# A GEGLU block on one core: the down projection of three pairs of hidden blocks by seven products for eight

## The chip, the core and the metric

The kernel runs on one core of a Trainium2 chip. A core has a matrix engine (TensorE, PE in the profile; PEld is its loading of weights), a vector engine (VectorE, DVE), a scalar engine (ScalarE, ACT), GpSimd (POOL) and a queue that issues transfers (SyncE, SP). Matrix products land in PSUM, eight banks of 128 partitions x 512 values of fp32, and are read from there by VectorE and ScalarE. The metric is the device time of one execution in microseconds; three runs of the kernel before gave 1671.05 us as their median (1670.72 to 1672.84).

## The reference

The block is a transformer layer on 2048 rows of 512 values, with 32 heads of attention over the last 512 keys and then a gated feed-forward part. `mod` holds six rows of 512 made from a condition vector; `gb` is the last of them.

```python
h = _layernorm(x, axis=-1) * (1 + ca) + sa
x = x + ga * _A_ref(h, A_k_cache, A_v_cache, A_wq, A_wo)     # attention
h = _layernorm(x, axis=-1) * (1 + cb) + sb
x = x + gb * _B_ref(h, B_w_gate, B_w_up, B_w_down)

def _B_ref(x, w_gate, w_up, w_down):
    g = jnp.einsum("bsd,df->bsf", x, w_gate)
    u = jnp.einsum("bsd,df->bsf", x, w_up)
    h = _gelu(g) * u
    return jnp.einsum("bsf,fd->bsd", h, w_down)
```

The hidden width is 1376. The change is in the last line of `_B_ref`, the down projection.

## The kernel before

**Numbers.** All products of fp32 values are made from fp16 parts: an operand is split into a high part (a rounding to fp16) and a low part (the rest), and a product of two operands is three matmuls, high x high, high x low and low x high. So what is called a product below is always three matmuls for each block of the inner dimension. The splits are an `activation` with Copy on ScalarE for the high part and a subtraction for the low part.

**Tiling of the feed-forward part.** The 2048 rows are four groups of 512 (`qg`), taken in two pairs `p` = 0 and 1. The hidden width is cut into NF = 11 blocks `f` of 128, of which the last, block 10, has 96. A unit `(p, f)` makes the hidden values of one block for the 1024 rows of a pair, transposed: 128 hidden values on the partitions, rows along the free dimension. The gate and up projections of a unit are made with Winograd's form of Strassen's scheme, seven products where a plain 2 x 2 scheme has eight, in four stages (`stage(u, k)`, k = 0 to 3), 42 matmuls of 512 columns in all. `finish(u, r)` multiplies the gelu by the up values for each of the two groups r on VectorE, and `hid_high` and `hid_low` split the result into the tile `hid`.

**The down projection.** Hidden blocks are taken two at a time. Once both units of such a couple are done, `down_put` puts eight entries into a list `DQ`, one for each of the pair's eight tiles of 128 rows. `down` takes one entry after each stage of the units that follow: `down_mm` issues six matmuls (two blocks, three each) of 512 columns, `hid` as the weights that are loaded and `w_down` as the operand that streams, into one bank of psO or psW, and `down_add` adds the bank to the accumulator of that tile of rows, `acc[t]`, on VectorE (one SCALAR_TENSOR_TENSOR of 128 x 512). The last addition of a tile is followed by its output transfer. `w_down` is loaded once, gated with `gb` and split once (`wd_load`, `wd_gate`, `wd_high`, `wd_low`), and kept.

The units come in the order of `UNITS`: all of p = 0 with p = 1's blocks 6 to 9 among them, then (0, 10), then (1, 0) to (1, 5), and (1, 10) last. So the couples (0, 1), (2, 3) and (4, 5) of p = 1 are made last, over the final 110 us or so. At the very end there are the couple (4, 5) and block 10 for all eight tiles: for tiles 4 to 7 of the pair the couple's and block 10's matmuls go into one bank and are added once, for tiles 0 to 3 they are two groups.

**Who sets the order.** The program does not run in the order in which it is written. The class `Weaver` records every call, lets a planner with costs for each engine play the whole program through, and issues the instructions of each engine in the order that it found. Each engine then works through its list strictly in that order, and waits on semaphores where an operand isn't there yet or a buffer isn't free. A low part or a sum written with `tt` may go to GpSimd or VectorE, as the planner chooses. All instructions stand on line 418, the call in `Weaver.issue`, so the profile's rows are told apart by the names of tiles: `psS` holds the units' products, `psO`, `psW` (two banks) and `psQ` the down projection's, `aw` the gate and up weights, `hid` the hidden values, `wd` w_down, `r` and `h` what lies between, `acc` the accumulators.

## Time and profile before

| | |
|---|---|
| median of three runs | 1671.05 us (1670.72 to 1672.84) |
| profiled execution, its own time | 1670.47 us |
| its span, first to last instruction | 1668.7 us |
| mean granted clock of TensorE | 0.998 |
| TensorE busy | 1658.7 us, 99% of the span |
| VectorE, ScalarE, GpSimd busy | 1265.9, 1220.4, 1232.5 us |

A row of a group in the profile reads: engine, operation, output <- inputs, count | busy time in all and mean ns of one | idle time of the engine ahead of these instructions, and what ended it. A row of the timeline gives start, duration, engine, operation, shapes, count, and in brackets the idle time before it. The duration of a matmul reaches to the end of its way through the array, so a stream of them goes faster than their durations say; the pitch of the weight loads shows the rate.

### The profile page before, as it was taken

How to read it: one execution, taken by the hardware profiler on the slowest of the kernel's cores; microseconds unless marked ns; L12 is line 12 of the kernel's file. 1: busy time of each engine (PE TensorE's matmuls, PEld its weight loads, DVE VectorE, ACT ScalarE, POOL GpSimd, SP SyncE). 2: the span in 40 equal slices, each digit the busy share in tenths (PEclk: the TensorE clock that was granted, in tenths of full speed). 3: DMA queues.
4: the chain of work that ended last, by engine and by line, in shares of the span. 5: the costliest groups of instructions: out<-in, count | busy, mean ns of one | idle time of the engine just before them, and what ended most of it. 6: DMA issues, size and time to landing. Idle time of an engine off the chain costs nothing.

```text
span 1668.7 us, 24116 instructions
## 1 busy us (share of the span) xinstructions
PE 1658.7 (99%) x7750; PEld 765.0 (46%) x7750; DVE 1265.9 (76%) x2374; ACT 1220.4 (73%) x2423; POOL 1232.5 (74%) x1013
## 2 busy tenths in 40 slices
PE   8999999999999999999999999999999999999999
PEld 5444444444444444444444444444444444444444
DVE  7877777778787877787888888777777966665555
ACT  6977778877877777878787878687777876545541
POOL 4878898867675767676666789999867898875530
PEclk9999999999999999999999999999999999999999
DMA  8778679977677767786989787879777712111111
GB/s 239 143 142 152 114 123 177 180 133 161 134 148 126 146 121 149 125 149 122 175 183 195 164 163 163 153 152 184 139 141 138 137 41 64 42 30 34 34 38 51
DMA packets 666351, 217.11 MB, mean 130 GB/s; under 512 B 581552, under 2 KB 648112, under 8 KB 666224
## 3 DMA queue, kind: packets, MB, share of 16 engines
q1 hardware_dynamic: 666224, 215.57, 65.0%
q8 instruction: 61, 1.00, 0.3%
q14 instruction: 66, 0.54, 0.1%
HBM read 68.68 MB, written 4.19 MB: 44 GB/s over the span
## 4 chain that ended last, share of the span: by engine, by line
PE 98%; DVE 1%; ACT 1%; DMA 0%; SPq 0%; issue 0%; DVEq 0%
PE psS L418 32%; PE psW L418 24%; PE psO L418 23%; PE psQ L418 18%; DMA wm<-in_w_mod_dram 0%; SPq L418 0%; ACT acc L418 0%; DVE st L418 0%; DVE acc L418 0%; ACT B L418 0%; ACT p L418 0%; DVE sc L418 0%; DVE q L418 0%; DVE mx L418 0%; ACT h L418 0%
## 5 line engine op out<-in xcount | busy, mean ns | idle before, releaser
L418 POOL TENSOR_TENSOR pp<-p,pp 128x1024 f16<-128x1024 f32 x256 | 545.4, 2130 | 269.8 <-ACT pp L418 161.7
L418 ACT ACTIVATE p<-psS,st,es 128x512 f32<-128x512 f32 x512 | 393.0, 773 | 168.0 <-DVE st L418 167.1
L418 DVE SCALAR_TENSOR_TENSOR acc<-psW,st,acc 128x512 f32<-128x512 f32 x496 | 367.9, 742 | 120.5 <-PE psW L418 118.7
L418 PE MATMUL psW<-wo,oT 128*128 128x512 f16 x1536 | 415.1, 379 | 0.0
L418 PE MATMUL psS<-kT,q 128*128 128x512 f16 x1536 | 383.9, 379 | 0.0
L418 PE MATMUL psO<-pT,v 128*128 128x512 f16 x1536 | 374.0, 379 | 0.0
L418 DVE TENSOR_REDUCE st<-psS 128x2 f32<-128x1024 f32 x256 | 312.7, 1221 | 60.3 <-PE psS L418 59.5
L418 ACT ACTIVATE pp<-p 128x1024 f16<-128x1024 f32 x256 | 271.2, 1059 | 3.8
L418 PEld LDWEIGHTS <-v 128*128 128x128 f16 x1536 | 150.2, 98 | 180.4 <-issue 0.5
L418 PEld LDWEIGHTS <-oT 128*128 128x128 f16 x1536 | 150.3, 98 | 180.1
L418 PEld LDWEIGHTS <-q 128*128 128x128 f16 x1536 | 147.5, 98 | 170.9 <-issue 1.1
L418 ACT ACTIVATE oT<-psO 128x512 f16<-128x512 f32 x128 | 76.0, 594 | 88.6 <-PE psO L418 88.1
L418 PE MATMUL psQ<-B,A 128*128 128x512 f16 x528 | 128.8, 380 | 0.1
L418 PEld LDWEIGHTS <-aw 128*128 128x128 f16 (+1 forms) x840 | 84.3, 100 | 96.0
L418 PE MATMUL psS<-T,aw 128*128 128x512 f16 (+1 forms) x480 | 116.3, 379 | 0.0
L418 PEld LDWEIGHTS <-A 128*128 128x128 f16 x756 | 74.5, 99 | 89.4 <-issue 1.9
L418 PE MATMUL psQ<-T,S 128*128 128x512 f16 x468 | 113.7, 379 | 0.0
L418 DVE SCALAR_TENSOR_TENSOR oT<-psO,oT 128x512 f16<-128x512 f32 x128 | 88.1, 689 | 32.9 <-ACT oT L418 32.6
L418 ACT ACTIVATION_READ_ACCUMULATOR p<-psS,st,es 128x1 f32 x512 | 101.5, 198 | 0.0
L418 PEld LDWEIGHTS <-S 128*128 128x128 f16 x624 | 61.0, 98 | 73.6
L418 DVE TENSOR_TENSOR r<-psS,h 128x512 f32<-128x512 f32 (+1 forms) x60 | 40.9, 688 | 69.5 <-ACT h L418 37.2
L418 DVE TENSOR_REDUCE mx<-raw 128x1 f32<-128x512 f32 x128 | 85.9, 675 | 9.5 <-DMA raw<-in_A_k_cache_dram 4.7
(210 smaller groups left out, 2264.6 us busy)
## 6 DMA issues: line engine op xcount, KB each, us to landing
raw<-in_A_k_cache_dram SPq DMA_DIRECT2D x32, 256.0 KB, 3.8
raw<-in_A_wq_dram SPq DMA_DIRECT2D x32, 256.0 KB, 3.3
raw<-in_A_v_cache_dram SPq DMA_DIRECT2D x32, 256.0 KB, 3.2
raw<-in_A_wo_dram SPq DMA_DIRECT2D x32, 256.0 KB, 3.0
pT<-pp SPq DMA_TRANSPOSE x512, 3.2
raw<-in_B_w_gate_dram SPq DMA_DIRECT2D x24, 256.0 KB, 3.1
raw<-in_B_w_up_dram SPq DMA_DIRECT2D x24, 256.0 KB, 3.1
raw<-in_B_w_down_dram SPq DMA_DIRECT2D x20, 256.0 KB, 2.9
```

The source lines that it names most:

```text
L418: made[n] = real(*a, **k)
```

## The change

For p = 1, the couples (0, 1), (2, 3) and (4, 5) (`PAIRS`) make the down projection in the same form of seven products for eight. The 2 x 2 scheme is: two groups of 512 rows, by two hidden blocks, by two halves of 256 output columns. One product is a matrix of 128 hidden values x 512 rows with a matrix of 128 x 256 of w_down.

- `finish` for these units only writes the multiplied values to a tile `hf` of fp32 (both groups). `pa_split` and `pa_sums` make from them the seven operands A11, A12, A22, S1 to S4: four sums of 128 x 512 and seven splits. They live in the tiles B11, T2, T1, B22 and so on of the gate and up part, which are free by then; for the couple (2, 3) in slots of `hid`.
- `wt_make` loads the two blocks of `w_down` again, gates them, makes the four differences of halves on GpSimd or VectorE, and splits the result into a tile `WT` (T3, T4 and B21 by couple).
- `pair_step` issues one step n of `CHAIN` for one half j of the rows (two tiles of 128): six matmuls of 256 columns into a bank that holds two tiles by 256 columns, and one addition on VectorE of 128 x 2 x 256 into a quarter of the result. There are two banks for each j, psW and psO for j = 0 and psW and psQ for j = 1. The steps 0, 2, 4 and 6 add up in one of them and 1; 3 and 5 use the other; a step that goes on in a bank waits until the addition of the step before has read it.
- For the last couple (`LAST`) the chain has ten steps in the order 0, 1, 2, 3, 4, 5, 7, 8, 6, 9. Steps 6 to 9 carry block 10: step 6 adds it to the seventh product's bank, 7, 8 and 9 have block 10 alone. They end with the output transfers, of 2 x 128 rows by 256 columns.
- The accumulators become one tile of 128 x 16 x 512, so that an addition can reach two tiles of rows. Scale factors are shifted by powers of two, and a count in the planner goes by columns.

In numbers of instructions: 168 matmuls of 512 columns go (with their 168 weight loads), 300 of 256 columns come. Additions on VectorE are 112 for 92.

```diff
@@
-HID = 2.0 ** 38
+HID = 2.0 ** 40
@@ def done
-        return sum(1.0 if ends[n] < until else 0.0 for n, e in enumerate(by) if e == "PE" and self.ops[n][3] == N)
+        return sum(self.ops[n][3] / N if ends[n] < until else 0.0 for n, e in enumerate(by) if e == "PE" and self.ops[n][3] > P)
@@
-    acc = [base.tile([P, D], F32, name=f"acc{t}", tag=f"acc{t}") for t in range(SQ // P)]
+    rows_ = base.tile([P, SQ // P, D], F32, name="acc")
+    acc = [rows_[:, t, :] for t in range(SQ // P)]
@@
+    PAIRS = {(1, f) for f in (0, 2, 4)}
...
+    def pa_split(p, f, nm):
+        src = {"A11": (f, 0), "S3": (f, 1), "A12": (f + 1, 0), "A22": (f + 1, 1), "S1": (f + 1, 1), "S2": (f, 0),
+               "S4": (f + 1, 0)}[nm]
+        t, v = pa_part(p, f, nm), HF[p, src[0]][:, src[1], :]
+        nc.scalar.activation(t[:, 0, :], v, AF.Copy)
+        tt(t[:, 1, :], v, t[:, 0, :], OP.subtract)
+
+    def pa_sums(p, f):
+        (a11, a21), (a12, a22) = [[HF[p, f + k][:, r, :] for r in range(2)] for k in range(2)]
+        pa_split(p, f, "A12")
+        pa_split(p, f, "A22")
+        tt(a22, a21, a22, OP.add)
+        tt(a21, a11, a21, OP.subtract)
+        tt(a11, a22, a11, OP.subtract)
+        pa_split(p, f, "S1")
+        pa_split(p, f, "S3")
+        tt(a12, a12, a11, OP.subtract)
+        pa_split(p, f, "S2")
+        pa_split(p, f, "S4")
+
+    def wt_make(f):
...
+            nc.sync.dma_start(t, w_down[(f + k) * P:(f + k + 1) * P, :])
+            tt(t, t, gb, OP.mult)
...
+    CHAIN = (("A11", 0, 0, 0, 0), ("A12", 1, 0, 0, 0), ("S2", 1, 1, 1, 0), ("S3", 0, 1, 1, 1), ("S1", 0, 0, 1, 1),
+             ("A22", 1, 0, 1, 0), ("S4", 1, 1, 0, 1), (None, 0, 1, 1, 1), (None, 0, 0, 0, 0), (None, 0, 0, 1, 0))
+    NEW = {0: 0, 1: 1, 3: 1, 7: 1, 8: 1, 9: 1}
+    LAST = (1, 4)
+
+    def pair_step(p, f, n, j):
+        nm, k, half, r, c = CHAIN[n]
+        if n in NEW:
+            PX["d", NEW[n], j] = bank(("psW", ("psO", "psQ")[j])[NEW[n]], (2, 1)[NEW[n]])
+        pd = PX["d", int(n in (1, 3, 5, 7, 8, 9)), j].rearrange("p (t c) -> p t c", t=2)
...
+                for i, (x_, y_) in enumerate(((0, 0), (0, 1), (1, 0))):
+                    nc.tensor.matmul(pd[:, t, :], a[:m, x_, js], w[:m, y_, :], start=n in NEW and (t, o, i) == (0, 0, 0),
+                                     stop=(o, i) == (len(ops) - 1, 2), skip_group_check=True)
+        g = 8 * p + 4 * r + 2 * j
+        v = rows_[:, g:g + 2, HALF[c]]
+        nc.vector.scalar_tensor_tensor(v, pd, ffs[:, 5:6], v, op0=OP.mult, op1=OP.add)
+        if ends:
+            nc.sync.dma_start(out[g * P:(g + 2) * P, :].rearrange("(t p) d -> p t d", p=P)[:, :, HALF[c]], v)
@@ def finish
+        if (p, f & ~1) in PAIRS:
+            if u not in HF:
+                HF[u] = right.tile([P, 2, N], F32, name="hf", tag="p32", bufs=2)
+            nc.vector.scalar_tensor_tensor(HF[u][:, r, :], t[:, 1, :], ffs[:, 4:5], t[:, 0, :], op0=OP.mult, op1=OP.mult)
+            if r == 0:
+                if f % 2 == 0:
+                    pa_split(p, f, "A11")
+                else:
+                    pa_sums(p, f - 1)
+            return
@@ the units' loop
+        if u in PAIRS:
+            wt_make(f)
         for k in range(4):
             stage(u, k)
             down()
...
-            if u == UNITS[-2]:
-                down_put(p, (h, h + 1), (0, 1, 2, 3))
+            if (p, h) in PAIRS:
+                DQ.extend((p, "pair", (h, n)) for n in ((0, 1, 2, 3, 4, 5, 7, 8, 6, 9) if (p, h) == LAST else range(7)))
             elif u != UNITS[-1]:
                 down_put(p, (h, h + 1) if h + 1 < NF else (h,))
     down(len(DQ))
-    pds = {}
...
-    down_put(1, (NF - 1,), (0, 1, 2, 3))
-    down(4)
```

Up to about three quarters of TensorE's list its order is the same as before. What it issues behind the last stage of the last unit, before; each of these matmuls stands three times with its weight load, for the three parts, and the sequence goes through tiles of rows, of which three are shown (wd 3101, 3129 and 3220 are the blocks 4, 5 and 10, hid 3379 and 3380 the two groups of block 4):

```order
L418 MATMUL psW_3410<-wd_3101,hid_3380 128x512
L418 MATMUL psW_3410<-wd_3129,hid_3392 128x512
L418 MATMUL psO_3414<-wd_3101,hid_3379 128x512
L418 MATMUL psO_3414<-wd_3129,hid_3391 128x512
L418 MATMUL psO_3414<-wd_3220,hid_3403 128x512
L418 MATMUL psO_3418<-wd_3220,hid_3404 128x512
```

And now, the chain of the couple (4, 5) in the order of its steps, j = 0 but for the second row; each stands six times with its load (B11, T2, T1 and B22 now hold A and S operands, B21 the new weights, wd 3086, 3114 and 3205 are the blocks 4, 5 and 10):

```order
L418 MATMUL psW_3409<-wd_3086,B11_1_3382 128x256
L418 MATMUL psW_3410<-wd_3086,B11_1_3382 128x256
L418 MATMUL psO_3411<-wd_3114,T2_1_3392 128x256
L418 MATMUL psW_3409<-B21_1_3370,T1_1_3393 128x256
L418 MATMUL psO_3413<-B21_1_3370,B11_1_3382 128x256
L418 MATMUL psO_3413<-B21_1_3370,T2_1_3392 128x256
L418 MATMUL psO_3415<-wd_3205,hid_3407 128x256
L418 MATMUL psO_3417<-wd_3205,hid_3408 128x256
L418 MATMUL psW_3409<-wd_3114,B22_1_3394 128x256
L418 MATMUL psO_3419<-wd_3205,hid_3407 128x256
```

Behind the last stage stand 99 matmuls of 512 columns before, and 150 of 256 now. The bank psW_3409 carries four steps, with an addition on VectorE to be waited for between each.

VectorE's list before, from the addition that ends the last unit's stages (`r<-psS`) on, in part:

```order
L418 TENSOR_TENSOR r_3396<-psS_3394,h32_3398 96x512
L418 SCALAR_TENSOR_TENSOR acc15_85<-psO_3405,ffs_95,acc15_85 128x512
L418 SCALAR_TENSOR_TENSOR r_3396<-r_3396,ffs_95 96x512
L418 SCALAR_TENSOR_TENSOR acc8_78<-psW_3406,ffs_95,acc8_78 128x512
L418 SCALAR_TENSOR_TENSOR r_3401<-r_3401,ffs_95 96x512
L418 SCALAR_TENSOR_TENSOR acc9_79<-psW_3407,ffs_95,acc9_79 128x512
L418 TENSOR_TENSOR hid_3403<-r_3401,hid_3403 96x512
```

And now, the same addition and what stands from the multiply `r_3404` on, some rows of evictions between them left out:

```order
L418 TENSOR_TENSOR r_3399<-psS_3397,h32_3402 96x512
L418 SCALAR_TENSOR_TENSOR acc_70<-psQ_3412,ffs_80,acc_70 128x2x256
L418 SCALAR_TENSOR_TENSOR B21_1_3370<-raw_3369,ffs_80,B21_1_3370 128x512
L418 SCALAR_TENSOR_TENSOR r_3404<-r_3404,ffs_80 96x512
L418 SCALAR_TENSOR_TENSOR acc_70<-psW_3409,ffs_80,acc_70 128x2x256
L418 SCALAR_TENSOR_TENSOR acc_70<-psO_3413,ffs_80,acc_70 128x2x256
L418 TENSOR_TENSOR hid_3407<-r_3404,hid_3407 96x512
L418 SCALAR_TENSOR_TENSOR r_3399<-r_3399,ffs_80 96x512
L418 SCALAR_TENSOR_TENSOR acc_70<-psQ_3414,ffs_80,acc_70 128x2x256
L418 SCALAR_TENSOR_TENSOR acc_70<-psO_3415,ffs_80,acc_70 128x2x256
L418 TENSOR_TENSOR hid_3408<-r_3399,hid_3408 96x512
```

Behind the first row there are 21 instructions before and 28 now; the last unit's multiplies and low parts have moved from the front of the stretch to its middle and end.

GpSimd's list before ends with the low parts of the last unit's gate and up weights (`aw`):

```order
L418 TENSOR_TENSOR aw_3369<-raw_3329,aw_3369 128x384
L418 TENSOR_TENSOR aw_3369<-S2f_3366,aw_3369 128x192
L418 TENSOR_TENSOR aw_3369<-S1f_3365,aw_3369 128x192
L418 TENSOR_TENSOR aw_3369<-S3f_3367,aw_3369 128x192
L418 TENSOR_TENSOR aw_3369<-S4f_3368,aw_3369 128x192
L418 TENSOR_TENSOR aw_3369<-raw_3330,aw_3369 128x192
```

Now the operands of the last couple stand behind them:

```order
L418 TENSOR_TENSOR aw_3367<-S4f_3366,aw_3367 128x192
L418 TENSOR_TENSOR B11_1_3382<-hf_3381,B11_1_3382 128x512
L418 TENSOR_TENSOR raw_3369<-raw_3369,raw_3368 128x256
L418 TENSOR_TENSOR raw_3369<-raw_3369 128x256
L418 TENSOR_TENSOR hf_3391<-hf_3381,hf_3391 128x512
L418 TENSOR_TENSOR hf_3381<-hf_3381 128x512
L418 TENSOR_TENSOR hf_3381<-hf_3391,hf_3381 128x512
L418 TENSOR_TENSOR T1_1_3393<-hf_3381,T1_1_3393 128x512
L418 TENSOR_TENSOR T1_1_3393<-hf_3391,T1_1_3393 128x512
L418 TENSOR_TENSOR hf_3391<-hf_3391,hf_3381 128x512
L418 TENSOR_TENSOR B22_1_3394<-hf_3391,B22_1_3394 128x512
```

The splits (names with two equal ends) and the sums (`hf`) take turns, and each sum needs the one before.

55 lines of the change are left out of this document (47 added, 8 removed).

## The prediction

> **What bounds the kernel now.** I read the page's busy shares first, then what TensorE waits for, then the last third of the span by stage, then single rows of its end.
>
> ```profile
> PE 1658.7 (99%) x7750; PEld 765.0 (46%) x7750; DVE 1265.9 (76%) x2374; ACT 1220.4 (73%) x2423; POOL 1232.5 (74%) x1013
> ...
> PE 98%; DVE 1%; ACT 1%; DMA 0%; SPq 0%; issue 0%; DVEq 0%
> ...
> PE psO L418 <- DVE acc L418: 0.4, 1, 0.4
> ```
>
> The second row is the chain that ended last: TensorE alone. The third is the only wait of TensorE from 1380 us to the end: 0.4 us in 289. So until here nothing but the number and length of its matmuls sets the time, and a removed matmul is worth its full length as long as no new wait stands in its place. The stages (core 0; PE, PEld, DVE, ACT, POOL busy, clock, DMA share, GB/s):
>
> ```profile
> 1550.00:1600.00 50.00, 50.00 (x233) 22.67 (x232) 29.53 (x43) 26.09 (x54) 30.26 (x41) 1.00 0.13 45
> 1600.00:1640.00 40.00, 40.00 (x187) 18.86 (x186) 22.43 (x33) 14.26 (x27) 5.24 (x9) 1.00 0.02 7
> 1640.00:1669.00 29.00, 24.63 (x115) 11.27 (x112) 16.09 (x24) 1.94 (x3) 0.00 (x0) 0.99 0.20 73
> ```
>
> The clock is full, the queues carry little, and VectorE, ScalarE and GpSimd are at 50 to 60% and fall off towards the end. All that the change adds goes into these stages, so what matters is whether the cover there is as wide as it looks. The very end, row by row:
>
> ```profile
> 1657.99 6.15 PEld L418 LDWEIGHTS <-hid 128*128 128x128 f16 x29
> 1659.29 1.46 PE L418 MATMUL psW<-wd,hid 96*128 96x512 f16 x6
> 1659.49 0.75 DVE L418 SCALAR_TENSOR_TENSOR acc<-psO,ffs,acc 128x512 f32<-128x512 f32 x1 [4.43 <-PE psO L418]
> 1660.15 1.40 DVE L418 SCALAR_TENSOR_TENSOR acc<-psW,ffs,acc 128x512 f32<-128x512 f32 x2
> 1663.82 0.81 PE L418 MATMUL psO<-wd,hid 96*128 96x512 f16 x3
> 1664.72 0.74 DVE L418 SCALAR_TENSOR_TENSOR acc<-psO,ffs,acc 128x512 f32<-128x512 f32 x1
> ```
>
> From these I take four prices. A matmul of 512 columns with its weight load: 29 loads in 6.15 us, the last 0.10 long, so 6.05/28 = 0.216 us. One eviction of VectorE in a row of several: 1.40 - 0.74 = 0.66 us. From a matmul's last column to the eviction that reads it: the last matmul starts at 1663.82 + 2 x 0.216 = 1664.25, streams to 1664.47, and is read from 1664.72: 0.21 to 0.25 us. And the drain: last eviction ends at 1665.46, the span at 1668.7, so 3.2 us for the last output transfer. Ahead of 1659.49 VectorE stands idle for 4.4 us; it is far from a bound there.
>
> **The change, part by part.** TensorE first. The three pairs of blocks and block 10 of the second pair of row groups lose 168 matmuls of 512 columns (3 x 48 + 24) and get 300 of 256 (3 x 84 + 48). In columns that is 18 x 512 less. The trace has no matmul of 256 columns, so its price is bounded. From below by half of 0.216, 0.108: fixed parts can't be smaller. From above by the load and the stream one after the other, 0.098 + 0.108 = 0.206, if nothing overlaps. The rows nearest to it are a weight load behind a short matmul:
>
> ```profile
> 1380.11 0.27 PE L418 MATMUL psQ<-ident,T 128*128 128x128 f32 x1
> 1380.11 0.21 PEld L418 LDWEIGHTS <-aw 128*128 128x128 f16 x2
> 1380.21 0.38 PE L418 MATMUL psS<-B,aw 128*128 128x512 f16 x1
> 1382.53 0.66 PE L418 MATMUL psQ<-ident,T 128*128 128x128 f32 x4
> 1384.97 0.60 PE L418 MATMUL psQ<-ident,T 128*128 128x128 f32 x4
> ...
> L418 PEld LDWEIGHTS <-hid 128*128 128x128 f16 x480 | 47.0, 98 | 56.1 <-issue 0.7
> ```
>
> The load for the next matmul begins when the one before it begins (1380.11 both), and that next matmul begins 0.10 us later: the load's 98 ns and hardly more. So a pair of load and matmul can follow each 0.10 to 0.11 us, and 256 columns need 0.108. Four transposes of 128 columns in a row, whose loads are of the slower 32-bit kind, keep a pitch of (0.60 - 0.27)/3 = 0.11 us, in the other row (0.66 - 0.27)/3 = 0.13. I take 0.109, by the row that has the same kind of load. Then 300 x 0.109 = 32.8 against 168 x 0.216 = 36.3: **-3.5 us** (ends: -3.9, and +25.5 with no overlap, which these rows rule out).
> The Trainium skill ("TensorE: Matmul & The Clock Gate", section "Wait — 56ns, not 53.3ns?") has a rule that speaks against the change: with the hardware's decoder off, firmware spends about 62 ns on each matmul. If a weight load cost as much again, an estimate by that page is 124 ns a pair, and the TensorE term would be +0.9 instead of -3.5 us; the 0.10 us between 1380.11 and 1380.21 doesn't bear it out, though one pair alone may have been decoded ahead.
>
> VectorE: 112 evictions for 92, since each product is added to one or two quarters of the result on its own: +20. Six weight roundings (low parts) come, twelve low parts of the hidden block move to GpSimd. Net +14 instructions, 14 x 0.66 = +9 us over the last 110 us. In the windows from 1550 to 1640 that is cover enough (52 of 90 us busy). At the end it is not. I count from the last matmul of the last unit's four stages, where in the changed order 150 matmuls of 256 columns are left: 150 x 0.109 = 16.4 us for TensorE. Behind the addition that reads that last matmul VectorE has 28 instructions, 29 with it, 29 x 0.66 = 19.1 us. Before, the same stretch held 99 matmuls of 512 (21.4 us) and 21 instructions of VectorE after that addition. So **the bound changes hands there**. In time: TensorE's last column would fall at 1664.47 - 3.5 = 1660.96 with no wait, the stages' last matmul at 1660.96 - 16.4 = 1644.6; VectorE begins its 29 at 1644.8 and is done at 1644.8 + 19.1 + 0.1 = 1664.0 at the earliest, against 1660.96 + 0.2 + 0.7 = 1661.9 if TensorE set it: **+2.1 us**. The banks force it upon TensorE: each pair of halves lives in one of two banks of psW and in psO and psQ, and step n+2 writes on in the bank that step n's eviction still reads.
>
> Inside those 19 us VectorE also waits once for another engine. The last unit's hidden block takes the way multiply (VectorE), high part (ScalarE), low part (VectorE), and the matmuls of block 10 wait for it:
>
> ```profile
> 1645.93 0.74 DVE L418 SCALAR_TENSOR_TENSOR r<-r,ffs 96x512 f32<-96x512 f32 x1
> 1646.59 0.74 DVE L418 SCALAR_TENSOR_TENSOR acc<-psW,ffs,acc 128x512 f32<-128x512 f32 x1
> 1646.71 0.63 ACT L418 ACTIVATE hid<-r 96x512 f16<-96x512 f32 x1 [1.95 <-DVE r L418]
> 1647.37 0.69 DVE L418 TENSOR_TENSOR hid<-r,hid 96x512 f16<-96x512 f32 x1
> ```
>
> 0.74 + 0.63 + 0.69 = 2.1 us with the two handovers; before, it was done by 1650.5, 8 us ahead of need, now its multiplies stand 8 and 17 places behind the stages' end, and in the changed order only one or two evictions lie between its links. Between 0 (all covered) and 2 x 2.1 I take **+0.6 us**, near the lower end, since there are evictions to run meanwhile.
>
> GpSimd and ScalarE: per pair 7 splits in two halves (ScalarE Copy 0.63, GpSimd subtraction), 4 sums, and for the weights 2 gates and 4 half-wide differences. On GpSimd that is 21 low parts, 12 sums, 6 gates and 12 half-wide differences, while 12 scalings go over to ScalarE: with the prices below at most 39 x 1.29 + 12 x 0.75 = 59 us. I cost it at nothing: from 1550 to 1655 GpSimd stood idle for 20 + 35 + 15 = 70 us; if that cover goes, TensorE waits for the sums (rival below). The prices it goes by:
>
> ```profile
> L418 POOL TENSOR_TENSOR T<-hf,T 128x512 f16<-128x512 f32 x6 | 7.8, 1306 | 2.9 <-DVE r L418 2.9
> L418 POOL TENSOR_TENSOR hf<-hf,ft 128x512 f32<-128x512 f32 x2 | 2.5, 1274 | 0.0
> L418 POOL TENSOR_TENSOR aw<-S4f,aw 128x256 f16<-128x256 f32 x11 | 8.3, 751 | 4.4 <-DVE hid L418 3.6 <-DVE r L418 0.7
> out_dram<-acc SPq DMA_DIRECT2D x9, 256.0 KB, 2.1
> ```
>
> Six more loads of w_down (256 KB each) lie in a stage where the queues are at 13%: nothing. The last output transfers carry as many bytes in rows half as long; between 0 and another 2.1 us I take +0.1, since the bytes are the same. One tile for all accumulators changes names, not waits; new scale factors are other constants: nothing.
>
> Sum: -3.5 + 2.1 + 0.6 + 0.1 = **-0.7 us** on the span: 1668.7 to 1668.0. The profiled execution took 1670.47, 0.6 below the median of the three runs, 1671.05. On that median: **1670.3 us**. Some 0.2% (3.3 us) is about what a measurement of this kernel can tell from no change.
>
> **Rivals.** *All of the gain arrives.* VectorE keeps up because evictions run earlier than I count, and the end follows TensorE: -3.5 + 0.1 gives 1667.6 us, just past 0.2%. For it: 4.4 us of idle VectorE before 1659.49. Against it: 29 instructions of 0.66 in 16.4 us don't fit in any order.
>
> *GpSimd is late: slower.* In the last pair the sums begin when both halves of block 5 are multiplied, by my count 6 us after the last unit's first stage (the two multiplies are the 8th and 9th of VectorE's instructions from there, 9 x 0.66). From there GpSimd does two low parts, a half-wide difference, three sums and three low parts in a row, 8 x 1.27 + 0.75 = 10.9 us, then a sum, ScalarE's Copy and the last low part, 1.27 + 0.63 + 1.3 = 3.2 us more: ready at 17 and 20 us. TensorE wants these operands at about 19 and 23.5. So there are 3 us of slack, after a stretch in which GpSimd is more than 80% busy by count (from the weights of the unit of block 2 on, 41 instructions of some 1.2 us and 40 narrow ones of 0.65: 75 us of work in 88). If it comes 7 us late at the end, or 2.5 us past its slack at each of the three pairs, TensorE waits 4 to 7 us: 1670.3 + 4 to 7 = 1674 to 1677 us. It decides from 4 us of waits upward (1670.3 + 4.1 is the 0.2% bound). Against it: GpSimd's own waits in this stretch before are mostly for ScalarE, it isn't backed up.
>
> *Short pairs can't follow at 0.109: slower.* If the 300 pairs go at the 0.13 us of the dearer row of transposes, TensorE's stream is 300 x 0.021 = 6.3 us longer than I count, and VectorE's surplus of 2.1 us covers so much of it: 1670.3 + 4.2 = 1674.5 us. From 0.127 us a pair on it is slower by over 0.2%. Against it stands the load of the right kind, 0.10 us. The firmware rule of the Trainium skill would be a cause of it.
>
> **How the numbers follow.** The forecast (the gain given back to VectorE at the end) 0.66; all of the gain 0.08; GpSimd late 0.20; dear pairs 0.06. Faster 0.08 (the first rival), same 0.66 (the forecast), slower 0.26 (the last two). Range: from 1667.5 (all gained) to 1676.0, which leaves out the far end of the GpSimd case; the forecast alone gives 1668.5 to 1673.0, from waits of 0 to 4.2 us where I took 0.6.
>
> **What would show it.** Matmuls 128x256 at a pitch of 0.109 in the weight loads' rows; 16.4 us of them behind the last stage, stretched to 18 or 19 by waits of psW, psO and psQ for VectorE's acc, each 0.1 to 0.9 us, 2 to 3 us in total; evictions 128x2x256 of 0.74 us standing back to back to the end; no waits of TensorE for GpSimd. Wrong if TensorE waits in the middle of the units (from 1550 on), or if the evictions in two pieces are dearer than those of 512 in one: at a pitch of 0.80 for 0.66 the end moves by 24 x 0.14 = 3.4 us.

## The result

The changed kernel takes 1673.2 us (median of 21 executions, 1672.66 to 1676.85), the kernel before on the same chip 1670.78 us (21 executions). The ratio is 1.0016, with a 95% interval of 1.001 to 1.0022: the change costs 2.4 us. The forecast was 1670.3 us. The profiled execution took 1672.93 us, its span is 1671.1 us against 1668.7 before. The executions of a kernel can lie in two groups: here 15 of 21 take 1672.7 to 1673.7 us and six 1674.3 to 1676.9, and in the spliced kernel below six of 11 take 1671.2 to 1672.0 and five 1673.0 to 1673.5.

What the change was for did happen. First the busy times, then weight loads of the last stretch (start, duration, engine, operation, count):

```profile
PE 1656.4 (99%) x7882; PEld 777.5 (47%) x7882; DVE 1273.7 (76%) x2384; ACT 1240.3 (74%) x2454; POOL 1279.5 (77%) x1052
```

```profile
1646.64 2.06 PEld L418 LDWEIGHTS <-hid 128*128 128x128 f16 x18
1648.71 1.30 PEld L418 LDWEIGHTS <-B 128*128 128x128 f16 x12
```

TensorE is busy 2.3 us less. Twelve loads of 0.10 us in 1.30 us are a pitch of (1.30 - 0.10)/11 = 0.109 us: a matmul of 256 columns with its load costs what was forecast, and 300 of them for 168 of 0.216 are worth the -3.5 us. VectorE has 7.8 us more, where the forecast had 9. So 5.9 us must have come from somewhere. I cut the span at two points which both kernels have: the opening ends with the first matmul psO<-pT,v (50.56 us before, 50.57 after), and the last matmul of the last unit's stages gives way to the next one at 1643.10 before and 1646.85 after. The rows that begin there, before and then after:

```profile
1643.10 0.81 PE L418 MATMUL psO<-wd,hid 128*128 128x512 f16 x3
1646.85 1.47 PE L418 MATMUL psW<-wd,hid 128*128 128x256 f16 x12
```

| | before | after | difference | of it less or more TensorE work | rest |
|---|---|---|---|---|---|
| opening | 50.56 | 50.57 | 0.0 | 0 | 0.0 |
| from there to the last stage's end | 1592.54 | 1596.28 | +3.74 | +1.5 | +2.2 |
| from there to the span's end | 25.60 | 24.25 | -1.35 | -5.0 | +3.7 |

The work column comes from the counts of matmuls: behind the last stage stand 99 of 0.216 us (21.4 us) before and 150 of 0.109 (16.4 us) now, so -5.0 us there; the whole change is -3.5, so +1.5 lies ahead. The last column is what is lost: 2.2 us ahead of the last stage's end and 3.7 us behind it. With -3.5 that is the measured +2.4.

**The loss upstream.** All waits of TensorE between 1280 and 1500 us in the changed kernel (what waits, for what: us in total, times, longest):

```profile
PE psQ L418 <- ACT hf L418: 1.2, 1, 1.2
PE psS L418 <- ACT r L418: 0.5, 1, 0.5
PE psS L418 <- DVE r L418: 0.3, 1, 0.3
```

In the kernel before there is one wait of 0.4 us there. The stretches (PE, PEld, DVE, ACT, POOL busy, clock, DMA share, GB/s), of the kernel before and then of the changed one:

```profile
1280.00:1400.00 120.00, 120.00 (x586) 58.34 (x585) 91.72 (x169) 93.56 (x175) 103.42 (x103) 1.00 0.45 89
1400.00:1500.00 100.00, 99.59 (x465) 45.33 (x463) 63.96 (x85) 52.45 (x100) 78.17 (x84) 1.00 0.15 41
```

```profile
1280.00:1400.00 120.00, 118.83 (x578) 57.37 (x577) 88.35 (x164) 95.33 (x178) 99.88 (x97) 1.00 0.44 87
1400.00:1500.00 100.00, 99.11 (x462) 45.12 (x461) 59.04 (x80) 55.62 (x106) 82.89 (x90) 1.00 0.16 42
...
1600.00:1640.00 40.00, 40.00 (x247) 24.64 (x246) 26.26 (x39) 19.54 (x36) 35.50 (x41) 1.00 0.16 59
```

TensorE loses 1.17 + 0.48 = 1.65 us of busy time in two stretches that lie ahead of the first matmul of the new scheme (it starts at 1585 us). A wait costs some 0.16 us more than that shows, since a single matmul of 512 columns is recorded with 0.38 us and takes 0.216 in a stream; with two waits more than before that makes 2.0 of the 2.2 us, as an estimate. In the stretch where GpSimd has most of its new work, 35.50 of 40 us, TensorE loses nothing. What happens at the 1.2 us wait can be read row by row. The kernel before, where the scaling of normalized rows (`hf<-psQ`, which empties the bank for the next four transposes) is done by VectorE:

```profile
1344.13 0.60 PE L418 MATMUL psQ<-ident,B 128*128 128x128 f32 x4
1344.84 0.81 DVE L418 TENSOR_SCALAR hf<-psQ,cols 128x512 f32<-128x512 f32 x1 [0.92 <-PE psQ L418]
1345.70 0.66 PE L418 MATMUL psQ<-ident,B 128*128 128x128 f32 x4
```

And the changed kernel, where the same scaling is on ScalarE's list, behind a load of its tables (which the kernel before has too, at 1344.54) and another read of products:

```profile
1344.83 0.60 PE L418 MATMUL psQ<-ident,B 128*128 128x128 f32 x4
1344.97 1.28 ACT L418 ACT_TABLE_LOAD   x1
1346.27 0.69 ACT L418 ACTIVATE r<-psS,ffs 128x512 f32<-128x512 f32 x1
1346.86 0.77 ACT L418 ACTIVATE hf<-psQ,cols 128x512 f32<-128x512 f32 x1
1347.68 0.66 PE L418 MATMUL psQ<-ident,B 128*128 128x128 f32 x4 [1.17 <-ACT hf L418]
```

The bank is full at 1345.43 and is read only from 1346.86. The diff touches no line of this part. The planner plays the whole program through, and for the changed program it found another order, in which such a scaling changes its engine.

**The loss at the end.** TensorE's waits from 1640 us on, in the changed kernel:

```profile
PE psQ L418 <- DVE acc L418: 0.7, 1, 0.7
PE psW L418 <- DVE acc L418: 0.5, 2, 0.3
PE psW L418 <- DVE B L418: 0.4, 1, 0.4
PE psO L418 <- DVE hid L418: 0.2, 1, 0.2
PE psO L418 <- DVE acc L418: 0.2, 1, 0.2
```

All are for VectorE. (One weight load, at 1653.72 us, is listed as waiting 0.62 us for GpSimd's T; but GpSimd was done with it at 1653.12, and what ended at 1653.67 was VectorE's rounding B.) Some of VectorE's rows, and the last wait it causes, in order of time:

```profile
1647.08 0.68 DVE L418 TENSOR_TENSOR r<-psS,h 96x512 f32<-96x512 f32 x1
...
1650.85 2.27 POOL L418 TENSOR_TENSOR T<-hf,T 128x512 f16<-128x512 f32 x2
...
1652.33 1.34 DVE L418 SCALAR_TENSOR_TENSOR B<-raw,ffs,B 128x512 f16<-128x512 f32 x1
...
1661.01 0.74 DVE L418 SCALAR_TENSOR_TENSOR acc<-psO,ffs,acc 128x512 f32<-128x512 f32 x1
1661.14 0.82 PE L418 MATMUL psQ<-wd,hid 96*128 96x256 f16 x6 [0.71 <-DVE acc L418]
...
1666.38 1.40 DVE L418 SCALAR_TENSOR_TENSOR acc<-psW,ffs,acc 128x512 f32<-128x512 f32 x2
```

From 1647.08 to 1661.67 VectorE works through 21 instructions with no gap but one of 0.14 us. TensorE does 102 matmuls between 1646.85 and 1661.14, 11.1 us of work in 14.3 us. (The list of waits adds up to 2.0 us only; each of the six costs 0.16 us more, as a matmul of 256 columns is recorded with 0.27 us for its 0.109, which makes 3.0 of them, as an estimate.) From 1661.14 on it goes without a wait: 48 matmuls in 5.25 us, to 1666.39. Then come two additions (1667.78; before, one stood behind the last column) and 3.3 us for the last output transfer. So of the 3.7 us, 3.2 are waits, 0.4 the second addition and 0.1 the transfer.

### The profile page after: what moved, and what is told of

Its sections match the earlier page's. It is cut to its first block, busy times and chain, and to the rows that moved or that the text cites. A ratio compares the mean times of both kernels' runs of the same rounds, so it can differ in the third digit from the quotient of the medians.

```text
span 1671.1 us, 24477 instructions
## 1 busy us (share of the span) xinstructions
PE 1656.4 (99%) x7882; PEld 777.5 (47%) x7882; DVE 1273.7 (76%) x2384; ACT 1240.3 (74%) x2454; POOL 1279.5 (77%) x1052
## 4 chain that ended last, share of the span: by engine, by line
PE 96%; DVE 1%; ACT 1%; issue 0%; SPq 0%; DMA 0%; POOL 0%; DVEq 0%
PE psS L418 32%; PE psW L418 24%; PE psO L418 22%; PE psQ L418 18%; DVE acc L418 0%; SPq L418 0%; DMA wm<-in_w_mod_dram 0%; ACT acc L418 0%; DVE st L418 0%; POOL B L418 0%; DVE mx L418 0%; ACT B L418 0%; DVE sc L418 0%; ACT p L418 0%; DVE h L418 0%
```

## The experiments

Theory A after the result: 2.2 us are the price of the new order ahead of 1500 us, an accident of the planning, and 3.7 us are VectorE's list at the end; the seven products themselves bring their 3.5. Against it stand, in several forms, that the operands of the new scheme (GpSimd's sums) come late, or that the end would absorb whatever is won upstream.

Many of the kernels below hold part of the order. The planner can be given starts and engines for instructions, and then only orders the rest; the edit is always

```diff
 class Weaver: issue()
-        span, keep, cut = None, {}, 0.0
-        for stop in self.CUTS:
+        span, keep, cut = None, kept(), KEEP_TO
+        for stop in (None,):
```

where `kept()` gives the start and the engine that the plan of one of the two kernels has for each instruction. Where it covers only what is planned ahead of 1500 us, the end is planned anew, and two such kernels can differ in more than the edit; four of the kernels (the spliced one, the two with instructions cut short, and the last) have their whole order given. Times are medians of 11 executions unless said otherwise, beside 15 to 33 of the kernel before in the same session (1670.7 to 1670.9 us).

### The changed kernel with the old order ahead of 1500 us

`kept()` holds what the kernel before plans ahead of 1500 us; all else is the changed kernel, and what lies behind is planned again.

> The change as it is, but every instruction that the planner started ahead of its 1500 us is held to the order of the kernel before (all engines); only what comes behind is planned anew. Theory A (of the 2.4 us lost, 2.1 come from waits of TensorE that the new plan has ahead of 1500 us, the rest from the end): 1673.2 - 2.1 = 1671.1 us, no wait of TensorE for ACT hf, ACT r or DVE r between 1280 and 1500 us, the end as in the changed kernel (TensorE's last matmul 19.5 us after the last unit's last one). Rival B (all is lost at the end, the earlier waits only move there): 1672.7 to 1673.4 us.

Measured: 1673.21 us, ratio 1.0016 (1.0007 to 1.0025). By the time alone B. The profile shows that the comparison was not the one meant. The stretches (columns as above):

```profile
1280.00:1400.00 120.00, 120.00 (x586) 58.33 (x585) 91.50 (x170) 95.08 (x177) 103.47 (x102) 1.00 0.46 92
```

The waits upstream are gone, and from the opening's end to the last stage's end it takes 1593.4 us for 1596.3. But the end had been planned anew too, and worse: 27.35 us for 24.25, with 159 matmuls behind the last stage (150 in the changed kernel), and with the last four additions in a row, three of them behind the last matmul's columns (1667.68):

```profile
1667.24 0.75 DVE L705 SCALAR_TENSOR_TENSOR acc<-psO,ffs,acc 128x512 f32<-128x512 f32 x1 [1.22 <-PE psO L705]
1667.90 0.74 DVE L705 SCALAR_TENSOR_TENSOR acc<-psQ,ffs,acc 128x512 f32<-128x512 f32 x1
1668.56 1.40 DVE L705 SCALAR_TENSOR_TENSOR acc<-psW,ffs,acc 128x512 f32<-128x512 f32 x2
```

So two things had changed, and the time could not tell them apart. The spliced kernel below holds both. (This profile is of an execution of 1675.24 us, 2.0 above the median; its opening took 52.73 us, 2.2 longer than the changed kernel's, so the stretches behind the opening can be compared.)

### The kernel before with the new order ahead of 1500 us

The kernel before, with no seven products anywhere; `kept()` holds what the changed kernel plans ahead of 1500 us.

> The kernel before, no product saved, but held to the changed kernel's order ahead of 1500 us. Theory A: 1670.8 + 2.1 = 1672.9 us, with the three waits between 1280 and 1500 us of the changed kernel. Rival B: 1670.8 us, the order ahead of 1500 us costs nothing.

Measured: 1674.0 us, ratio 1.002 (1.0011 to 1.0029), 3.1 us slower than before. The same three waits stand in it with the same lengths, and the same stretches:

```profile
1280.00:1400.00 120.00, 118.83 (x578) 57.26 (x576) 88.14 (x163) 95.33 (x178) 100.37 (x97) 1.00 0.44 88
1400.00:1500.00 100.00, 99.11 (x462) 45.10 (x460) 59.23 (x81) 55.66 (x106) 82.79 (x90) 1.00 0.15 42
```

Up to the last stage's end it is 2.3 us later than before. Theory A holds: the order alone, with none of the new work, costs what was missing upstream. Another 1.0 us came from the time between the last addition and the span's end, 4.3 us for 3.2. In this profile the last output transfer lands 3.3 us after its issue, where no output transfer of the kernel before takes more than 2.1. The last 13 packets come one after the other, as from one of the 16 DMA engines alone, and the last part lands 1.06 us behind the others. Among the output's packets there is one of another kind, a load of instructions of 8 KB, which the kernel before does not have there (the rate from 1655 to 1680 us in 40 slices, then queue, kind, packets, MB and share):

```profile
GB/s 0 0 0 0 0 0 0 0 0 0 0 0 0 118 374 380 377 69 377 370 374 370 383 151 23 3 0 0 0 0 0 0 0 0 0 0 0 0 0 0
q14 instruction: 1, 0.01, 0.1%
```

That this load held up the one engine is read from one profile and was not tested.

### Two of the three couples

The couples (0, 1) and (2, 3) by seven products, the couple (4, 5) and block 10 as before; old order ahead of 1500 us.

```diff
-    PAIRS = {(1, f) for f in (0, 2, 4)}
+    PAIRS = {(1, f) for f in (0, 2)}
...
+            elif u == UNITS[-2]:
+                down_put(p, (h, h + 1), (0, 1, 2, 3))
...
+    pds = {}
...
```

> Old order ahead of 1500 us as in e1; only the couples (0, 1) and (2, 3) by seven products, the last couple and block 10 as before. Theory A (a couple in the middle of the units is worth its columns, 6 x 0.216 less the short matmuls' fixed part = 1.2 us; only the end is bound by VectorE): 1670.8 - 2.4 = 1668.4 us. Rival C (GpSimd and VectorE are too full for the splits and evictions in the middle as well): 1670.3 us or more, with waits of TensorE between 1550 and 1640 us.

Measured: 1668.47 us, ratio 0.9987 (0.9978 to 0.9995): 2.5 us faster than before. In TensorE's work it has 96 x 0.216 - 168 x 0.109 = 2.4 us less, and that is what arrives. No wait of TensorE stands in its last stages, though GpSimd makes two thirds of the new operands there:

```profile
1500.00:1640.00 140.00, 140.00 (x717) 71.59 (x715) 86.91 (x119) 71.30 (x141) 96.73 (x118) 1.00 0.13 39
```

This kernel is faster than both.

### Three couples, the last chain in eight steps

Block 10 is added in the banks of steps 1, 5, 6 and 7 in place of steps of its own: the same matmuls, four additions of VectorE fewer. Old order ahead of 1500 us; 150 matmuls and 24 instructions of VectorE behind the last stage.

```diff
-            ... ((0, 1, 2, 3, 4, 5, 7, 8, 6, 9) if (p, h) == LAST else range(7))
+            ... ((0, 2, 3, 4, 5, 7, 6, 1) if (p, h) == LAST else range(7))
-        ends = (p, f) == LAST and n > 5
+        ends = (p, f) == LAST and n in (1, 5, 6, 7)
```

> Old order ahead of 1500 us; all three couples by seven; in the last chain block 10 is added into the banks of steps 1, 5, 6 and 7, in the order 0, 2, 3, 4, 5, 7, 6, 1, so that 8 steps stand for 10: the same matmuls, 4 evictions fewer. Theory A (the end is bound by VectorE's evictions): 4 x 0.66 = 2.6 us less than e1, of which TensorE's own stream allows some 2: 1668.7 to 1669.3 us. Rival D (TensorE waits at the end for operands, the splits on GpSimd and the last hidden block, not for evictions): as e1, 1671 us, or more, since block 10 is wanted earlier.

Measured: 1668.77 us, ratio 0.9988 (0.9979 to 0.9997). The stretch behind the last stage takes 22.3 us for 16.4 of matmuls; in the kernel before it was 25.6 for 21.4, in the changed kernel 24.25 for 16.4. Fewer additions, less loss: 5.9 us above the matmuls in place of 7.9. Its end was planned anew, though, so not all of this need come from the four additions: against the first experiment, from which the expectation reckons, it is 4.4 us less, more than the 2.6 us of four additions. TensorE also waits 0.3 us for GpSimd's T here, the only such wait in the last stretch of these profiles. It is also faster than both kernels, and cannot be told from the one with two couples.

### The changed kernel's own end behind the old order

`kept()` holds the order of the kernel before ahead of 1500 us and exactly that of the changed kernel behind it. This is the clean form of the first experiment.

> The changed kernel's instructions, with the order of the kernel before for everything planned ahead of 1500 us and exactly the changed kernel's order for everything behind it (150 matmuls and 29 instructions of VectorE behind the last stage, as in the changed kernel; the kernel with the old order tried first had its end planned anew, with 159 matmuls there). Theory A, the new order upstream costs 2.2 us between 1280 and 1500 us and up to 0.5 in the opening, on top of what the end costs: 1673.2 - 2.2 to 2.8 = 1670.4 to 1671.0; in the profile no wait of TensorE between 1280 and 1500, the last stage's last matmul 1594.0 us behind the opening's end (changed kernel 1596.25), and from there to the span's end 24.25 as in the changed kernel. Rival B, the end absorbs it, since VectorE and GpSimd set when the end is done and come no earlier: 1672.9 to 1673.4, with the stretch behind the last stage over 26 us.

Measured: 1671.98 us, ratio 1.0008 (0.9999 to 1.0017). The profile is of an execution of 1671.69 us. The stretch and, below it, the first of TensorE's waits from 1640 us on:

```profile
1280.00:1400.00 120.00, 120.00 (x586) 58.24 (x584) 91.50 (x169) 93.51 (x175) 103.42 (x102) 1.00 0.46 90
```

```profile
PE psW L733 <- DVE B L733: 0.7, 1, 0.7
```

From the opening's end to the last stage's end it takes 1594.4 us, 1.9 less than the changed kernel. Behind it 24.6 us, 0.35 more, for the wait on VectorE's rounding of B21 (`DVE B`) is 0.7 us in place of 0.4. Its opening was 0.35 us longer, in this execution. So 1.9 of the 2.2 us come back where A says, and 1.2 to 1.6 of them reach the end (1.2 by the median and by the span, 1.6 without the longer opening). B, that nothing arrives, falls; but A's figure of 1670.4 to 1671.0 was too low by 1 us or so.

### Four additions cut short

The changed kernel in exactly its own order; in the additions of steps 1 and 3 of the last chain

```diff
-        nc.vector.scalar_tensor_tensor(v, pd, ffs[:, 5:6], v, op0=OP.mult, op1=OP.add)
+        if (p, f) == LAST and n in (1, 3):
+            nc.vector.scalar_tensor_tensor(v[:, :, 0:1], pd[:, :, 0:1], ffs[:, 5:6], v[:, :, 0:1], op0=OP.mult, op1=OP.add)
+        else:
+            nc.vector.scalar_tensor_tensor(v, pd, ffs[:, 5:6], v, op0=OP.mult, op1=OP.add)
```

> The changed kernel in exactly its own order; the four additions of steps 1 and 3 of the last chain read and write 128x2x1 instead of 128x2x256. It leaves out all but one column in 256 of those additions. Matmuls, transfers, GpSimd and ScalarE are unchanged. Theory A, VectorE's count sets the end: four additions of 0.66 us become some 0.1 to 0.2, 1.8 to 2.2 us less on VectorE, all of it on the path: 1673.2 - 1.8 to 2.2 = 1671.0 to 1671.4. Rival B, the end is set by when operands are ready (GpSimd's sums, the hidden block's parts), and VectorE only follows: within 0.5 us of the changed kernel, 1672.7 to 1673.4.

Measured: 1671.71 us, ratio 1.0005 (0.9997 to 1.0014), 1.5 us less than the changed kernel. The stretch behind the last stage takes 22.9 us for 24.25. Rows of GpSimd and VectorE in it:

```profile
1650.96 2.73 POOL L734 TENSOR_TENSOR T<-hf,T 128x512 f16<-128x512 f32 x2
1651.13 0.21 DVE L734 SCALAR_TENSOR_TENSOR acc<-psO,ffs,acc 128x2 f32<-128x2 f32 x1
...
1651.89 0.77 DVE L734 SCALAR_TENSOR_TENSOR B<-raw,ffs,B 128x512 f16<-128x512 f32 x1
1652.59 1.64 DVE L734 SCALAR_TENSOR_TENSOR r<-r,ffs 96x512 f32<-96x512 f32 x1
```

The four rows give 4 x (0.66 - 0.2) = 1.8 us, of which 1.3 to 1.5 arrive. VectorE's list sets the end, as A says: the time is 0.3 us above A's range and 1.0 below B's. The rest was lost on the way: the instruction that now stands beside GpSimd's subtraction is another one, `r<-r`, and it takes 1.64 us where it took 0.74.

### The last couple alone

Only the couple (4, 5), with block 10 and all ten steps, by seven products; old order ahead of 1500 us.

```diff
-    PAIRS = {(1, f) for f in (0, 2, 4)}
+    PAIRS = {(1, 4)}
```

> Only the couple of blocks 4 and 5, with block 10, goes by seven products, in ten steps as in the changed kernel; the couples 0 to 3 as before; the order of the kernel before ahead of 1500 us. TensorE: 72 x 0.216 - 132 x 0.109 = -1.2 us. Behind the last stage stand 159 matmuls (132 of them of 256 columns, 20.2 us) and 30 instructions of VectorE (19.8 us). Theory A, the loss sits in the last chain and the couples before it bring their gain whole: at least the difference between the changed kernel's end and the gain, 1670.9 - 1.2 + 2 to 4 = 1671.7 to 1673.7, slower than before by itself, as the kernel with the first two couples alone was faster by 2.5. Rival B, the loss comes only where all three couples follow one another (GpSimd backed up): 1669.7 to 1670.2.

Measured: 1671.73 us, ratio 1.0003 (0.9994 to 1.0011), 0.9 us above the kernel before, just at A's lower bound, and 1.5 us above the upper bound of B. By its work it should be 1.2 us faster. Up to the last stage's end it is as fast as it should be (1592.5 us); behind it, it takes 26.8 us for 20.2 of matmuls, 6.6 above them where the kernel before has 4.2. TensorE waits for nothing there: its last column is through at 1663.34, 20.3 us behind the last stage. But the last four additions fall within 2.7 us, and the last of them ends 1.7 us behind that column (1.0 before):

```profile
1662.33 0.75 DVE L705 SCALAR_TENSOR_TENSOR acc<-psO,ffs,acc 128x512 f32<-128x512 f32 x1 [0.34 <-PE psO L705]
1663.00 0.74 DVE L705 SCALAR_TENSOR_TENSOR acc<-psQ,ffs,acc 128x512 f32<-128x512 f32 x1
1663.65 1.40 DVE L705 SCALAR_TENSOR_TENSOR acc<-psW,ffs,acc 128x512 f32<-128x512 f32 x2
```

and each sends 256 KB. The queues of the core are full from 1665 to 1668 us (336 to 348 GB/s), and the last transfer ends 4.75 us behind the last addition; before it was 3.2. So in this kernel 1.5 us of the loss are the output's transfers and 0.7 the row of additions behind the last column. The spacing of the four additions alone does not make the 1.5: in the first experiment the last four stand as close, and the span ends 3.5 us behind the last one. What this kernel has besides is a load of instructions of 16 KB among the output's packets, and one output transfer, at 1662.02 us, whose issue on SyncE took 1.68 us, where the others took 0.37 to 0.65; the last four were issued behind it, 0.3 to 0.7 us after their additions. Without that the time would be some 1.2 us less (4.75 - 3.5), 1670.5, as an estimate, above B's range and below A's. So this run does not decide between A and B. Where TensorE has 20.2 us of work and VectorE 30 x 0.66 = 19.8, VectorE doesn't hold it up.

### GpSimd's sums cut short

The changed kernel in exactly its own order; for the last couple the four sums work on two columns in 512 (one of the four is shown).

```diff
 def pa_sums
-        tt(a22, a21, a22, OP.add)
+        c = slice(0, 2) if (p, f) == LAST else slice(0, N)
+        tt(a22[:, c], a21[:, c], a22[:, c], OP.add)
...
```

> The changed kernel in exactly its own order; the four sums of the last couple's operands (GpSimd, 1.28 us each) work on two columns in 512, so GpSimd's chain from the first multiply of block 5 to the last operand is some 4 us shorter. It leaves out nearly all of these sums. Theory A, GpSimd's operands come in time and VectorE's list and the stage's late end set the time: within 0.5 us of the changed kernel, 1672.7 to 1673.7; the only gain would be VectorE's rounding of B21 that took 1.34 us beside GpSimd's subtractions in place of 0.74, if GpSimd is then done before it, -0.6. Rival B, GpSimd's chain of sums holds up TensorE behind the last stage (wait of its weight load for T, 0.6, and what follows): -1 to -3 us, 1670.2 to 1672.2.

Measured: 1672.91 us, ratio 1.0015 (1.0006 to 1.0023), 0.3 us below the changed kernel. GpSimd's four sums took 4 us less, and nothing of it came through but the row that A names: VectorE's rounding of B21 took 0.74 us, as GpSimd was done 0.12 us after its start. So GpSimd's operands were not what TensorE waited for. The profiled execution (1674.05 us) has something else in it, told at the end.

### Two couples, the whole order found anew

The kernel with the first two couples again, with the planner free from the start.

> The kernel with the first two couples alone, as measured at 1668.47, but with the whole program's order found anew, as in the changed kernel; TensorE's order is that of the changed kernel up to about 1250 us, VectorE's and ScalarE's differ from it in some places from the start. Theory A, the new order upstream costs what it cost twice already, whatever stands behind it (the waits of TensorE for hf and r between 1280 and 1500): 1668.5 + 2.2 to 2.8 = 1670.7 to 1671.3. Rival B, those waits belong to one particular order and a third one need not have them: 1668.0 to 1669.3.

Measured: 1669.24 us, ratio 0.9991 (0.9982 to 1.0). Between 1280 and 1500 us TensorE has one wait of 0.4 us, as before. Theory A, as it was put here, falls: the loss upstream does not belong to every order found anew. It belongs to the one that the planner found for the three couples. This third order costs some 0.7 us up to the last stage's end and 0.2 to 0.4 behind it. It has all other lines of the diff too (the one tile of accumulators, the scale factors, the count by columns), so these alone do not bring the waits.

### One scaling back on VectorE

The changed kernel's own order; one instruction, the scaling at 1346.86 us shown above, is moved to VectorE's list, between the two neighbours that it has in time.

```diff
 kept(), the entry of this one instruction
-    ScalarE, start as in the changed kernel
+    VectorE, start as in the kernel before
```

> The changed kernel in its own order but for one instruction: the scaling of normalized rows, hf<-psQ, that stands at 1346.86 us on ScalarE behind a load of its tables (1.28 us) and an r, goes back to VectorE, where the kernel before has it. VectorE has nothing to do from 1344.2 to 1347.0 there. Theory A, this one placement makes the wait of TensorE's transposes (psQ <- ACT hf, 1.2 us at 1347.68) and what it costs comes through to the end, since TensorE bounds all that follows up to the last stage: 1673.2 - 1.0 to 1.2 = 1672.0 to 1672.2, with PE busy 119.9 to 120.0 of 120 us between 1280 and 1400. Rival B, the wait only moves on to the next operand of this stretch, or the end absorbs it: 1672.8 to 1673.4.

Measured: 1672.56 us, ratio 1.0009 (1.0 to 1.0018), 0.6 us less than the changed kernel. The bank is now emptied in time, and the stretch (below) recovers most of its loss:

```profile
1345.97 0.81 DVE L734 TENSOR_SCALAR hf<-psQ,cols 128x512 f32<-128x512 f32 x1 [1.35 <-PE psQ L734]
1346.84 0.65 PE L734 MATMUL psQ<-ident,B 128*128 128x128 f32 x4
```

```profile
1280.00:1400.00 120.00, 119.71 (x583) 57.84 (x582) 90.06 (x165) 95.14 (x178) 99.89 (x98) 1.00 0.45 89
```

PE busy goes from 118.83 to 119.71, and the way to the last stage's end from 1596.3 to 1595.45 us: 0.85 of the 1.2 us. The other 0.3 turned into a second wait of 0.3 us for VectorE's `r`, which stands behind the scaling on its list. Between A and B: the time lies 0.36 us above A's range and 0.24 below B's, the stretch (119.71, where A has 119.9 to 120.0) nearer to A. One instruction on another engine, 240 us ahead of the first new matmul, is worth 0.6 to 0.85 us.

## Why the prediction was wrong

**The step that failed** is the one with no number. The sum has terms for TensorE's columns, VectorE at the end, the hidden block and the output transfers; everything ahead of the couples was taken at nothing without a word, and of the diff's other lines it was said that they change "names, not waits". TensorE's list was found the same up to about three quarters, and that was taken for the whole of it. In the two profiles VectorE's lists part at 87 us and ScalarE's at 107 us, and the planner plays the whole program. It costs 2.2 us. The kernel before with this order alone has the same three waits (e2); putting the old order back gives 1.9 of it back (e5), and putting one scaling back gives 0.85 (e10). The sign that the prediction named for itself, waits "in the middle of the units (from 1550 on)", looked in the wrong place: there are none from 1500 to 1640.

**TensorE's columns, -3.5:** right. The pitch is 0.109 us, and the kernel with two couples brings 2.5 us for 2.4. The rival of dear pairs falls with it. So does the estimate of 124 ns a pair, which let a weight load cost as much again as the 62 ns of firmware that the Trainium skill ("TensorE: Matmul & The Clock Gate", section "Wait — 56ns, not 53.3ns?") gives for a matmul with the hardware's decoder off: the rows show 109 for a stream of twelve and more. The 62 ns alone are less than that, and these rows do not test them.

**The bound changes hands at the end, +2.1 + 0.6 + 0.1:** the mechanism right, the size short. Measured are 3.7 us in place of 2.8. The row-by-row reading shows 21 instructions with one gap of 0.14 us and TensorE waiting for them; the run with four short additions (1.3 to 1.5 us less) shows the cause, and the one with eight steps agrees. Three things were mis-sized. The price of 0.66 us for each of the 29 leaves out what happens beside GpSimd: the B21 rounding took 1.34 us, whose extra 0.6 us are most of what was missing. The hidden block's handovers, taken at 0.6 us, show as 0.2 us of TensorE's waits and as no gap in VectorE's list that ends on ScalarE. And VectorE does not set the end down to its last instruction: it does so up to 1661.14 us, then TensorE's last 48 matmuls do, and two additions stand behind the last column. The prediction's inner range is also wrong in itself: with waits of 0 to 4.2 us in place of 0.6 the sum gives 1669.7 to 1673.9 us, and not 1668.5 to 1673.0.

**GpSimd at nothing:** right as far as its lateness goes. Its sums cut to nothing moved the time by 0.3 us, and the rival of a late GpSimd, to which I gave 0.20, falls. It cost something in a way that I did not think of, by the instruction of VectorE beside which it ran (B21's rounding; with the short additions `r<-r`).

**The output transfers, +0.1:** right for the changed kernel (3.3 for 3.2 us). In the last couple alone they cost 1.5 us, within the 2.1 that the prediction gave as a bound, but with an issue held up that it did not think of.

**The sum:** -3.5 + 3.7 = +0.2 would have been the time with the order unchanged, 1671.0; the spliced kernel gave 1671.98, and 1671.69 in its profiled execution, with 0.3 of the 2.2 us still lost upstream and a wait that is 0.3 us longer. The rest up to 1673.2 is the order upstream. The range held the time, the sign of the forecast was wrong. The sign would have been wrong by the end alone, where 0.9 us were missing and the forecast was -0.7. That the range held is luck as far as the 2.2 us go: nothing in the prediction bounds what another order can cost, and the two rivals that gave the range its upper part both fell.

What stays open: why the planner's choice falls otherwise for the three couples and not for two, and whether the loads of instructions make the 1.0 and the 1.2 us at the end of the two kernels in which they fall among the output's packets.

## What to carry to other kernels

Where a planner plays the whole program through, no part of it is out of a change's reach: compare the lists of all engines from their first instruction, or hold the order ahead of the change, before a term of nothing is written down. A saving on the engine that bounds the kernel arrives whole where the others have slack (2.5 us for 2.4 with two couples) and is lost where the saved time is the cover of another engine's list, here at the end; so in this kernel the scheme is best left out of the last stretch, or given fewer additions there. And a time alone does not tell what an experiment changed: the first run here agreed with the wrong theory because its end had been planned anew.

## What the runs showed of the hardware

**VectorE beside GpSimd.** An instruction of VectorE with both large operands in SBUF takes 0.74 us alone. In the changed kernel the B21 rounding starts at 1652.33, while GpSimd's two subtractions run until 1653.12, and ends at 1653.67, 0.55 behind them. With the short additions the rounding came earlier and took 0.77, and `r<-r`, started at 1652.59 beside the same subtractions (until 1653.69), ended at 1654.23, 0.54 behind them; GpSimd's pair took 2.73 us there, with the rounding in its midst, and 2.27 in the changed kernel. The additions that read PSUM, at 1651.01 and 1651.67 in the changed kernel, keep their 0.74 beside the same subtractions. With the sums cut short the rounding starts at 1652.40, 0.12 before GpSimd's end, and takes 0.74. The reverse shows as well. With the sums cut short, a GpSimd sum of two columns takes 0.20 us at 1646.41, but this one, begun while VectorE's `r<-r` runs (1653.06 to 1653.80), ends at 1653.86:

```profile
1653.22 0.64 POOL L734 TENSOR_TENSOR hf<-hf 128x2 f32<-128x2 f32 x1 [0.69 <-DVE B L734]
```

This looks like one of the two waiting until the other is done, and not like a shared speed; it is read from these rows, and was not tested by itself. The Trainium skill ("SBUF — State Buffer", section "SBUF: two separate sides") has such a rule: an instruction of VectorE with two inputs in SBUF and one of GpSimd that reads SBUF lock the same ports, and the one that starts second waits for the first. The rows agree with it.

**TensorE's clock fell to half in one profile.** In the profiled execution of the kernel with short sums the granted clock falls at the very end. The stretches (columns as above; the clock is the third from the right), then a row of the timeline within them:

```profile
1660.00:1662.00 2.00, 1.39 (x9) 1.09 (x9) 2.00 (x4) 0.56 (x1) 0.00 (x0) 0.78 0.00 0
1662.00:1664.00 2.00, 2.00 (x12) 1.42 (x10) 0.71 (x2) 0.00 (x0) 0.00 (x0) 0.50 0.68 230
1664.00:1666.00 2.00, 2.00 (x18) 1.68 (x17) 1.29 (x3) 0.00 (x0) 0.00 (x0) 0.87 0.37 126
```

```profile
1661.81 1.06 PE L734 MATMUL psW<-wd,hid 96*128 96x256 f16 x4
```

Four matmuls of 256 columns take 1.06 us there, and 0.60 in the changed kernel's profile. By the clock column the stretches hold some 3.4 us at half the clock, which is 1.7 us lost, and this execution was 1.1 us above the median of its kernel. The longest wait of TensorE between 1640 us and the fall was 0.71 us. The profiles of the changed kernel and of the one with one scaling moved have the same wait of 0.7 us there and keep the clock at 1.00, so the waits alone did not decide it. The Trainium skill ("TensorE: Matmul & The Clock Gate", section "A second HAM failure mode: psum-queue depth-cycling") tells of such a fall where TensorE idles briefly and often between groups of matmuls while it cycles through banks, there with the clock going to and fro; this profile agrees in that it shows one such fall, among short waits for banks.

**The opening varies.** TensorE's wait for the first normalized rows (psO <- ACT acc) is 0.6 us in the changed kernel's profile and 0.5 to 1.7 in the others, with the same instructions; the opening's end lies between 50.15 and 52.73 us. Differences of less than a microsecond between two profiles are therefore read from the opening's end on, as in the table above.
